# Hashed attention and two feed-forward stages: the second half's AV issued in one block, the next pair's mask moved behind a score

## Chip, core and metric

The program runs on one core of a Trainium2 chip. The metric is the device time of one execution in microseconds: 554.61 us before the change, the median of three runs (554.46 to 555.11). One execution was profiled; its own time is 554.77 us and the span of its trace, from the first to the last instruction, is 553.1 us.

## What is computed

Attention over 16 heads (2 x 8) of 768 tokens with head size 64, in which a query sees only the keys that fall into the same hash bucket, then a feed-forward block, then a mixture of eight experts. The change lies in the attention alone:

```python
q_bits = (einsum('bhsd,dk->bhsk', q, proj) > 0)      # 6 bits, k_bits likewise
mask = q_bucket[:, :, :, None] == k_bucket[:, :, None, :]
scores = where(mask, scale * matmul(q, k.T), -1e9)
attn = exp(scores - scores.max(-1)); attn /= attn.sum(-1) + 1e-9
out = matmul(attn, v)
```

The output of the heads, as a matrix of 1536 x 512, goes through `h = x @ w_in`, a softmax times h, a layer norm and `@ w_out`, and then through the experts; all of that stays as it was.

## The kernel before

The attention takes the first 205 us or so, the two feed-forward stages the rest. Everything is issued in an order written out by hand: each engine works through its own list, and only semaphores tie the lists together.

Heads go in pairs `j` = 0 to 7, one head in each half of the 128 partitions. A pair has two halves `i` of 384 queries (`HW`), and a half has six chunks `c` of 128 keys (`NC`). For every chunk `score(j, i, c)` (L278) puts eight matmuls (L252) into one PSUM tile: query and key in a high part (`Hq`, `Hk`) and a low part (`Lq`, `Lk`), and a fourth product of the hash features `Fq`, `Fk`, which adds a large number where buckets agree. ScalarE (ACT) writes the exponent of it to one of eight buffers `pt` (L288), and GpSimd (POOL) adds the exponents up for the softmax's denominator (L294, L296). For the row maximum `rowmax` (L256) computes the scores a second time, coarsely (four matmuls), and VectorE (DVE) reduces them (L264). Six of these make a half's maxima; `submax` (L266) sends them by DMA into a row of `Fq`, where they are subtracted in the fourth product. Row maxima run ahead: `scans(m)` in `run` issues the next m of them after each score, by a table of six numbers for each half.

`av(j, i, cs)` (L299) multiplies the exponents by the values (L305), two matmuls for each chunk, one for each head. All 12 of a half (24 in the trace) go to one PSUM tile, `self.xs`; `evac` (L310) then moves it out on ACT (L314, L318). Of PSUM there are four tiles of two banks in rotation (`self.order`). While an AV runs, two of them are taken out: `xs`, and `aside`, in which a piece of a feed-forward weight is taken apart (`convert`, `finish`: ACT L553, DVE L554, L557, L560, then ACT L577 or L569 and DVE L578 or L572). `norm` (L366) multiplies finished output by the reciprocal sums on DVE (L369): 768 columns, but only 384 in pair 1.

`first(j)` runs after chunk 1 of a pair's first half. It issues the AV of the second half of pair j-1, `mask(j + 1)` (L228: four matmuls L234 into two PSUM tiles, then `Fk` by ACT, L241, and `Fq` by DVE, L243) and `turn(j + 1)` (L175: `Hk` and `Hq`, L179, on ACT). `second(j)` does the same for the AV of the first half after chunk 1 of the second half, and makes the hash and the bits for pair j+2, which `mask` reads. `low` (L189) makes `Lk` and `Lq` on POOL.

The three row maxima of pair j+1 that follow in the first half of pair j need `Fk`, `Fq`, `Hk` and `Hq` of pair j+1.

Of the kernel before, what the change touches and what calls it, by code (L numbers as in the profile page):

```python
# [119 lines left out]
class Attention:  # L120
# [257 lines left out]
    def run(self, n, extra, fills):  # L378
        self.last = (n - 1, 1)
        scan = [(j, i, c, kh) for j in range(n) for i in range(2) for c in range(3) for kh in range(2)]  # L380

        def scans(m):
            for x in scan[:m]:
                self.rowmax(*x)
            del scan[:m]

        self.hash(0)
        self.turn(0)
        self.load(1, "qk")
        self.warm(8, cols=P)  # L390
        self.mask(0)
        self.warm(2, D)
        self.turn(1)
        for m in range(NC):
            scans(1)
            self.warm(1, D, HW)
        self.hash(1)
        self.submax(0, 0)
        self.threshold(1)
        scans(1)  # L400
        self.mask(1)
        scans(2)
        self.load(0, "v")
        next(extra)
        half = [tuple(range(NC)), (0, 1, 2), (3, 4, 5)]

        rest = []

        def convert():
            rest.extend(next(extra, []))  # L410
            if rest:
                rest.pop(0)()

        def finish():
            while rest:
                rest.pop(0)()

        def first(j):
            self.submax(j, 1)
            if j + 2 < n and j == 0:  # L420
                self.load(j + 2, "qk")
            if j:
                self.xs, self.aside = self.order[:2]
                del self.order[:2]
            if j:
                convert()
                self.av(j - 1, 1, (0, 1))
            if j + 1 < n:
                if j:
                    self.mask(j + 1)  # L430
                    self.turn(j + 1)
            if j:
                self.av(j - 1, 1, (2, 3, 4, 5))
                if j + 1 < n:
                    finish()
                    self.order += [self.xs, self.aside]
                else:
                    self.order.append(self.xs)
                self.norm(j - 1)
                self.evac(j - 1, 1)  # L440
                if j + 2 < n:
                    self.load(j + 2, "qk")
                if j + 1 < n:
                    self.load(j + 1, "v")
            if j == 0:
                self.load(1, "v")

        def second(j):
            if j + 1 < n:
                self.submax(j + 1, 0)  # L450
                self.low(j + 1, "k", self.nc.gpsimd)
                self.low(j + 1, "q", self.nc.gpsimd)
                fills.pop(0)()
            self.xs, self.aside = self.order[:2]
            del self.order[:2]
            convert()
            self.av(j, 0, half[0])
            if j + 1 < n:
                ps = self.wide()
                if j + 2 < n:  # L460
                    self.hash(j + 2, ps[:, 0])
                self.totals(j, ps[:, 1])
                if j + 2 < n:
                    self.threshold(j + 2)
                self.sums(ps[:, 1])
                if j:
                    finish()
                    self.order[1:] = [self.xs, self.order[1], self.aside]
                else:
                    self.order.append(self.xs)  # L470
            self.evac(j, 0)

        for j in range(n):
            for i in range(2):
                for c in range(NC):
                    self.score(j, i, c)
                    scans(((2, 1, 0, 1, 1, 1), (2, 1, 1, 1, 1, 0))[i][c])
                    if c == 1:
                        (second if i else first)(j)
                    if c == 3:  # L480
                        finish()
                        if j in (0, n - 1):
                            self.order.append(self.aside)
                    if (i, c) == (1, 4):
                        self.recip(j)
                    if (j, i) == self.last:
                        if c == 3:
                            ps = self.wide()[:, 0]
                            self.totals(j, ps)
                            self.sums(ps)  # L490
                        if c == 4:
                            self.aside = self.order.pop(0)
                            convert()
                            self.av(j, 1, half[1])
                        if c == 5:
                            finish()
                            self.order.append(self.aside)
        self.av(n - 1, 1, half[2])
        self.evac(n - 1, 1)
        self.order.sort(key=self.pools.index, reverse=True)  # L500
        self.direct(n - 1, 1)
        for ops in extra:
            for f in ops:
                f()
# [999 lines left out]
```

## Time and profile before

| quantity | value |
|---|---|
| median of three runs | 554.61 us |
| profiled execution, its own time | 554.77 us |
| its span | 553.1 us |
| TensorE (PE) busy | 541.9 us, 98% of the span |
| VectorE (DVE) busy | 388.7 us, 70% |
| GpSimd (POOL) busy | 326.5 us, 59% |
| ScalarE (ACT) busy | 268.7 us, 49% |
| granted TensorE clock, mean | 0.998 of full speed |

A share of busy time is an average over the whole program. The change moves instructions in the attention only, so what it is worth has to be read there, from the order of the instructions on each engine and the waits between them. The matmuls' weight loads have a lane of their own in the trace (PEld), and a gap there is the clearest sign that PE stood still, since the ends of matmuls are modelled.

### The profile page before, as it was taken

How to read it: one execution, taken by the hardware profiler on the slowest of the kernel's cores; microseconds unless marked ns; L12 is line 12 of the kernel's file. 1: busy time of each engine (PE TensorE's matmuls, PEld its weight loads, DVE VectorE, ACT ScalarE, POOL GpSimd, SP SyncE). 2: the span in 40 equal slices, each digit the busy share in tenths (PEclk: the TensorE clock that was granted, in tenths of full speed). 3: DMA queues.
4: the chain of work that ended last, by engine and by line, in shares of the span. 5: the costliest groups of instructions: out<-in, count | busy, mean ns of one | idle time of the engine just before them, and what ended most of it. 6: DMA issues, size and time to landing. Idle time of an engine off the chain costs nothing. (4 is left out here: it accounts for less than half of the span.)

```text
span 553.1 us, 9989 instructions
## 1 busy us (share of the span) xinstructions
PE 541.9 (98%) x3863; PEld 435.2 (79%) x3863; DVE 388.7 (70%) x789; ACT 268.7 (49%) x457; POOL 326.5 (59%) x268
## 2 busy tenths in 40 slices
PE   8899999999999999999999999999999999999995
PEld 4766677766677557888888888998989989899894
DVE  8878789798897667777678777766574663655731
ACT  3556758576676542322233324547346454463530
POOL 5498988989889942110001040347695875957741
PEclk9999999999999999999999999999999999999999
DMA  3555474454644338300000030349818458397201
GB/s 114 134 140 192 130 214 157 117 191 110 221 113 116 106 99 318 146 0 1 1 1 1 0 98 1 114 133 378 283 62 324 158 211 296 130 328 256 78 23 37
DMA packets 48550, 76.49 MB, mean 138 GB/s; under 512 B 11885, under 2 KB 20845, under 8 KB 48496
## 3 DMA queue, kind: packets, MB, share of 16 engines
q1 hardware_dynamic: 43360, 59.90, 33.7%
q10 hardware_dynamic: 2896, 9.57, 5.1%
q0 software_dynamic: 2240, 6.31, 3.3%
q8 instruction: 32, 0.52, 0.4%
q14 instruction: 22, 0.18, 0.1%
HBM read 58.79 MB, written 17.94 MB: 139 GB/s over the span
## 5 line engine op out<-in xcount | busy, mean ns | idle before, releaser
L1181 POOL TENSOR_TENSOR wl<-ws,wh 128x512 fp32r<-128x512 f32 x75 | 107.5, 1466 | 41.0 <-ACT wh L1179 41.0
L294 POOL TENSOR_TENSOR acc<-pt,pt 128x768 f32<-128x768 f32 x46 | 85.4, 1857 | 21.1 <-ACT pt L288 21.1
L264 DVE TENSOR_REDUCE m<-ps 128x2 f32<-128x768 f32 x96 | 88.5, 953 | 8.6 <-PE ps L252 6.1
L288 ACT ACTIVATE pt<-ps 128x768 f32<-128x768 f32 x96 | 76.5, 814 | 35.5 <-PE ps L252 35.4
L1291 PE MATMUL o<-wh,wo 128*128 128x512 f32 x256 | 82.6, 394 | 0.0
L1179 ACT CAST wh<-ws 128x512 fp32r<-128x512 f32 x120 | 66.4, 619 | 6.6 <-DMA ws<-in_moe_w_dram 3.5
L654 POOL TENSOR_TENSOR xl<-xT,xh 128x512 fp32r<-128x512 f32 x12 | 15.5, 1293 | 90.8 <-ACT xh L663 50.4
L305 PE MATMUL ps<-pt,v 128*64 128x385 f32 x384 | 67.2, 493 | 0.0
L1181 DVE TENSOR_TENSOR wl<-ws,wh 128x512 fp32r<-128x512 f32 x45 | 52.2, 1186 | 12.5 <-ACT wh L1179 12.4
L1275 DVE SCALAR_TENSOR_TENSOR wo<-g,wo 128x512 fp32r<-128x512 f32 x32 | 22.1, 691 | 52.6 <-ACT wo L1274 52.6
L296 POOL TENSOR_TENSOR acc<-acc 128x768 f32<-128x768 f32 x30 | 55.5, 1850 | 2.4
L1274 ACT ACTIVATE wo<-g 128x512 fp32r<-128x512 f32 x32 | 19.1, 598 | 75.4 <-PE g L1269 75.4
L1291 PEld LDWEIGHTS o<-wh,wo 128*128 128x128 f32 x256 | 48.1, 188 | 9.7
L305 PEld LDWEIGHTS ps<-pt,v 128*64 128x64 f32 x384 | 25.5, 136 | 31.6 <-issue 31.2
L1291 PE MATMUL o<-wl,wo 128*128 128x512 f32 x128 | 50.2, 392 | 0.0
L672 PE MATMUL h<-wi,xh 128*128 128x512 f32 x192 | 49.5, 399 | 0.0
L672 PE MATMUL y<-wo,lh 128*128 128x512 f32 (+1 forms) x176 | 40.8, 384 | 0.0
L672 PEld LDWEIGHTS h<-wi,xh 128*128 128x128 f32 x192 | 34.9, 188 | 7.4 <-ACT xh L663 0.6
L835 POOL DMA_INDIRECT scratch<-row,slot x12 | 12.0, 999 | 47.5 <-DVE slot L862 22.9
L672 PEld LDWEIGHTS y<-wo,lh 128*128 128x128 f32 x176 | 31.5, 188 | 6.6 <-issue 0.2
L252 PE MATMUL ps<-Hk,Hq 64*128 64x384 f32 x192 | 35.9, 357 | 0.9 <-DVE rb L348 0.4
L252 PE MATMUL ps<-Hq,Hk 64*128 64x384 f32 x192 | 36.0, 364 | 0.6 <-DVE wo L572 0.3
(246 smaller groups left out, 1148.0 us busy)
## 6 DMA issues: line engine op xcount, KB each, us to landing
ws<-in_moe_w_dram SPq DMA_DIRECT2D x32, 1024.0 KB, 9.6
scratch<-zero SPq DMA_DIRECT2D x7, 1030.0 KB, 7.3
r<-scratch SPq DMA_DIRECT2D x16, 257.5 KB, 2.9
raw<-in_moe_w_in_dram ACTq DMA_DIRECT2D x8, 512.0 KB, 5.5
raw<-in_moe_w_out_dram ACTq DMA_DIRECT2D x8, 512.0 KB, 5.8
v<-in_v_dram SPq DMA_DIRECT2D x8, 384.0 KB, 5.6
rd<-rd SPq DMA_DIRECT2D x16, 192.0 KB, 3.4
out_dram<-zero SPq DMA_DIRECT2D x3, 1024.0 KB, 6.6
```

The lines of the kernel that those rows point to most:

```text
L252: self.nc.tensor.matmul(ps[:, h], w[r], x[r], start=(n == 0), stop=(n == len(jobs) - 1), tile_position=(D * h, 0))
L264: nc.vector.tensor_reduce(out=st["m", i][:, c, :, kh], in_=ps, axis=AX.X, op=ALU.max, negate=True)
L288: nc.scalar.activation(out=pt[:, :, 0:HW], in_=ps, func=AF.Exp, scale=0.125)
L294: eng.tensor_tensor(out=acc, in0=st["pt", i, c - 1][:, :, 0:HW], in1=pt[:, :, 0:HW], op=ALU.add)
L296: nc.gpsimd.tensor_tensor(out=acc, in0=parts.pop(), in1=acc, op=ALU.add)
L305: nc.tensor.matmul(st["x", i][D * h:D * h + D, 0:HW + 1], st["v"][:, h, c, :], st["pt", i, c][:, h, 0:HW + 1], start=(c == 0), stop=(c == ...
L672: nc.tensor.matmul(ps, a[:, k, :], w[j](k), start=(n == 0), stop=(n == len(jobs) - 1))
L1179: nc.scalar.copy(hi[:, k, :], t[:, k, :])
L1181: eng.tensor_tensor(out=lo[:, k, :], in0=t[:, k, :], in1=hi[:, k, :].bitcast(F32), op=ALU.subtract)
L1274: nc.scalar.activation(out=hi, in_=ps, func=AF.Relu)
L1275: nc.vector.scalar_tensor_tensor(out=hl[:, 2 * g:2 * g + 2, :], in0=ps, scalar=0.0, in1=hi.bitcast(F32), op0=ALU.max, op1=ALU.subtract)
L1291: nc.tensor.matmul(st["o"][t], h[:, f, t * P:(t + 1) * P], w[:, f % 4, :], start=(f == 0 and n == 0), stop=(f == 7 and n == 2),)
```

## The change

In `first(j)` the AV of the second half of pair j-1 is issued as one block of 12 matmuls (24 in the trace, where each counts twice), where two chunks came ahead of the mask and four behind it. `turn(j + 1)` comes ahead of the AV as before. `mask(j + 1)` leaves `first` and is issued behind the score of chunk 2 of the first half. The table of row maxima of the first half, (2, 1, 0, 1, 1, 1), becomes (2, 1, 0, 0, 2, 1) for j over 0: the first one of pair j+1 now follows the score of chunk 4. It was behind chunk 3. Pair 0 is as it was, and pair 7 has no mask to make, so six masks are moved (those of pairs 2 to 7, in pairs 1 to 6).

```diff
             if j:
                 convert()
-                self.av(j - 1, 1, (0, 1))
-            if j + 1 < n:
-                if j:
-                    self.mask(j + 1)
+                if j + 1 < n:
                     self.turn(j + 1)
-            if j:
-                self.av(j - 1, 1, (2, 3, 4, 5))
+                self.av(j - 1, 1, half[0])
                 if j + 1 < n:
                     finish()
                     self.order += [self.xs, self.aside]
...
                 for c in range(NC):
                     self.score(j, i, c)
-                    scans(((2, 1, 0, 1, 1, 1), (2, 1, 1, 1, 1, 0))[i][c])
+                    if (i, c) == (0, 2) and 0 < j < n - 1:
+                        self.mask(j + 1)
+                    scans((((2, 1, 0, 0, 2, 1) if j else (2, 1, 0, 1, 1, 1)), (2, 1, 1, 1, 1, 0))[i][c])
```

`half[0]` is the tuple of all six chunks. The changed file is two lines shorter, so a line of Weights such as L560 is L558 there.

On PE, in the first half of pair 3, from the last row maximum ahead of the AV to the second score behind it (ps_1317 and ps_1318 are the mask's two tiles). Before:

```order
L252 MATMUL ps_1297<-Fk_1008,Fq_1010 128x384 x2
L305 MATMUL ps_1312<-pt6_101,v_723 64x385 x2
L305 MATMUL ps_1312<-pt7_102,v_723 64x385 x2
L234 LDWEIGHTS tab_170
L234 MATMUL ps_1317<-bits_1182,tab_170 128x384
...
L234 MATMUL ps_1318<-bits_1182,tab_170 128x384
L305 MATMUL ps_1312<-pt0_95,v_723 64x385 x2
...
L305 MATMUL ps_1312<-pt3_98,v_723 64x385 x2
L252 MATMUL ps_1354<-Hq_1014,Hk_1012 128x384 x2
...
L252 MATMUL ps_1364<-Hq_1014,Hk_1012 128x384 x2
```

With the change, at the same place (ps_1354 and ps_1355 are the mask's tiles here):

```order
L252 MATMUL ps_1297<-Fk_1045,Fq_1047 128x384 x2
L305 MATMUL ps_1316<-pt6_101,v_713 64x385 x2
...
L305 MATMUL ps_1316<-pt3_98,v_713 64x385 x2
L252 MATMUL ps_1344<-Hq_999,Hk_997 128x384 x2
...
L252 MATMUL ps_1344<-Fq_1047,Fk_1045 128x384 x2
L234 LDWEIGHTS tab_170
L234 MATMUL ps_1354<-bits_1182,tab_170 128x384
...
L234 MATMUL ps_1355<-bits_1182,tab_170 128x384
L252 MATMUL ps_1364<-Hq_999,Hk_997 128x384 x2
```

The mask left the AV, which is whole now, and stands between the scores of chunks 2 and 3.

On DVE, in the first half of pair 2, from the end of the weight piece to the row maxima of pair 3. Before:

```order
L560 SCALAR_TENSOR_TENSOR ps_992<-raw_838,ps_992 128x512
L243 CAST Fq_1010<-ps_1003 128x768
L578 TENSOR_TENSOR wi1_72<-ps_992,wi0_71 128x512
L369 TENSOR_TENSOR xT_67<-xr_717,rd_932 128x768
L264 TENSOR_REDUCE m0_103<-ps_1062 128x2
```

With the change:

```order
L558 SCALAR_TENSOR_TENSOR ps_992<-raw_838,ps_992 128x512
L576 TENSOR_TENSOR wi1_72<-ps_992,wi0_71 128x512
L369 TENSOR_TENSOR xT_67<-xr_707,rd_932 128x768
L243 CAST Fq_1047<-ps_1040 128x768
L264 TENSOR_REDUCE m0_103<-ps_1072 128x2
```

The copy that makes `Fq` moved behind the second half of the weight piece and behind the norm.

On ACT, in the same place, before:

```order
L553 ACTIVATE ps_992<-raw_838 128x512
L241 ACTIVATE Fk_1008<-ps_1002 128x768
L179 CAST Hk_1012<-k_711 128x768
L179 CAST Hq_1014<-q_709 128x768
L577 CAST wi0_71<-ps_992 128x512
```

With the change:

```order
L179 CAST Hq_999<-q_709 128x768
L575 CAST wi0_71<-ps_992 128x512
...
L318 ACTIVATE xr_1021<-ps_1001,vb_1019 128x384
L288 ACTIVATE pt2_97<-ps_1029 128x2x384
L241 ACTIVATE Fk_1045<-ps_1039 128x768
L288 ACTIVATE pt3_98<-ps_1049 128x2x384
```

The activation that makes `Fk` moved from ahead of the two casts to a place between the exponents of chunks 2 and 3. POOL's list and the queues' lists keep their order.

## Rows read from the trace of the kernel before

**Rows 1.** The page: busy time of each engine over the whole span.
```profile
PE 541.9 (98%) x3863; PEld 435.2 (79%) x3863; DVE 388.7 (70%) x789; ACT 268.7 (49%) x457; POOL 326.5 (59%) x268
```

**Rows 2.** Timeline of PEld (start us, us, engine, line): AV starts, pairs 1, 3, 6.
```profile
40.58 0.20 PEld L305 LDWEIGHTS ps<-pt,v 128*64 128x64 f32 x4 [0.19 <-issue]
...
87.34 0.20 PEld L305 LDWEIGHTS ps<-pt,v 128*64 128x64 f32 x4 [0.19 <-issue]
...
157.46 0.20 PEld L305 LDWEIGHTS ps<-pt,v 128*64 128x64 f32 x4 [0.19 <-issue]
```

**Rows 3.** Timeline of PEld, pair 3: mask, AV resumed, score of chunk 2.
```profile
88.78 0.11 PEld L234 LDWEIGHTS <-tab 64*128 64x128 bf16 x4 [0.60 <-issue]
89.21 0.20 PEld L305 LDWEIGHTS ps<-pt,v 128*64 128x64 f32 x4 [0.32 <-issue]
...
91.95 0.19 PEld L252 LDWEIGHTS ps<-Hq,Hk 64*128 64x128 f32 x2 [0.60 <-ACT Hq L179]
```

**Rows 4.** Timeline of PEld, pair 7: a whole AV block and the score behind it.
```profile
180.18 0.20 PEld L305 LDWEIGHTS ps<-pt,v 128*64 128x64 f32 x4 [0.18 <-DVE m L264]
...
184.21 0.19 PEld L252 LDWEIGHTS ps<-Hq,Hk 64*128 64x128 f32 x2 [0.60 <-issue]
```

**Rows 5.** Timeline of PE, pair 3: score 3, row maximum, score 1, second AV.
```profile
92.76 0.33 PE L252 MATMUL ps<-Hq,Hk 64*128 64x384 f32 x2
...
93.63 0.34 PE L252 MATMUL ps<-Fk,Fq 64*128 64x384 f32 x2
...
97.30 0.34 PE L252 MATMUL ps<-Hq,Hk 64*128 64x384 f32 x2
...
98.44 4.10 PE L305 MATMUL ps<-pt,v 128*64 128x385 f32 x24
```

**Rows 6.** Timeline of ACT, pair 3: two exponents; then behind the second AV.
```profile
93.02 1.52 ACT L288 ACTIVATE pt<-ps 128x768 f32<-128x768 f32 x2 [0.18 <-PE ps L252]
...
102.15 0.58 ACT L577 CAST wi<-ps 128x512 fp32r<-128x512 f32 x1 [2.44 <-DVE ps L560]
102.63 0.17 ACT L314 COPY vb<-ps 128x1 f32<-128x1 f32 x1
102.83 0.58 ACT L318 ACTIVATE xr<-ps,vb 128x384 f32<-128x384 f32 x1
```

**Rows 7.** Timeline of DVE, pair 3, from the weight piece to the row maxima.
```profile
90.31 0.72 DVE L560 SCALAR_TENSOR_TENSOR ps<-raw,ps 128x512 int32<-128x512 int32 x1
90.92 0.97 DVE L243 CAST Fq<-ps 128x768 fp32r<-128x768 f32 x1
92.10 0.69 DVE L578 TENSOR_TENSOR wi<-ps,wi 128x512 fp32r<-128x512 f32 x1 [0.22 <-ACT wi L577]
92.71 1.48 DVE L369 TENSOR_TENSOR xT<-xr,rd 128x768 f32<-128x768 f32 x1
94.11 5.74 DVE L264 TENSOR_REDUCE m<-ps 128x2 f32<-128x768 f32 x6
```

**Rows 8.** Timeline of POOL, pairs 3 and 4.
```profile
91.52 1.85 POOL L294 TENSOR_TENSOR acc<-pt,pt 128x768 f32<-128x768 f32 x1
94.68 1.85 POOL L294 TENSOR_TENSOR acc<-pt,pt 128x768 f32<-128x768 f32 x1 [1.31 <-ACT pt L288]
...
114.88 1.84 POOL L294 TENSOR_TENSOR acc<-pt,pt 128x768 f32<-128x768 f32 x1
```

**Rows 9.** Timeline of POOL and DVE, pair 5; then DVE behind the attention.
```profile
138.28 1.85 POOL L294 TENSOR_TENSOR acc<-pt,pt 128x768 f32<-128x768 f32 x1
139.62 1.32 DVE L369 TENSOR_TENSOR xT<-xr,rd 128x768 f32<-128x768 f32 x1
...
207.07 0.89 DVE L369 TENSOR_TENSOR xT<-xr,rd 128x768 f32<-128x768 f32 x1
```

**Rows 10.** Timeline of PE: the matmul behind the mask of pair 1, among row maxima.
```profile
16.38 0.51 PE L252 MATMUL ps<-Hk,Hq 64*128 64x384 f32 x2 [0.36 <-DVE m L264]
```

**Rows 11.** Timeline of PEld, the first score of pair 7.
```profile
177.69 0.19 PEld L252 LDWEIGHTS ps<-Lq,Hk 64*128 64x128 f32 x2 [0.35 <-POOL Lq L193]
```

## The prediction

> **What bounds the kernel now.** I read the page first, then the weight loads of the attention, then DVE, ACT and POOL around one AV block. TensorE is busy for 98% of the span [rows 1], so a change pays if it takes PE time away and costs if it makes PE wait. The attention repeats itself: the AV at the middle of the first half starts at 40.58 in pair 1 and at 157.46 in pair 6 [rows 2], five pairs later, 23.38 us each. One pair therefore stands for six. I take pair 3 and count from the start of its AV, at 87.34 [rows 2]. Three things are to be seen there.
>
> PE does not wait for data in this first half; it only changes over between kinds of matmul. The AV, split by the mask, takes 4.61 us up to the next score (91.95 [rows 3]), with gaps of 0.60, 0.32 and 0.60 in the weight loads. A whole block followed directly by a score takes 4.03 (180.18 to 184.21 [rows 4]).
>
> DVE is nearly full just behind it: weight piece, `Fq`, second part of the piece, norm, then six reductions with no gap from 94.11 on [rows 7]. Their step is 5.74 / 6 = 0.96. The third of them ends at 94.11 + 2.87 = 96.98, and the score that reuses its PSUM tile (chunk 1 of the second half) starts at 97.30 [rows 5]. So the reductions have 0.3 us of slack.
>
> The norm is held by POOL. It ends at 92.71 + 1.48 = 94.19, and POOL's addition, begun at 91.52, ends at 93.37 [rows 7, 8]: 0.82 later. In pair 5 the same difference is 139.62 + 1.32 - 138.28 - 1.85 = 0.81 [rows 9], though the norm started elsewhere. With POOL quiet a norm takes 0.89 [rows 9]. So the norm makes next to no progress while POOL adds, and its end is POOL's end plus 0.82.
>
> **The change, part by part.**
>
> *The AV in one block.* It saves 4.61 - 4.03 = 0.58 for each of six pairs. The mask's own matmuls come back among the scores. PE streams them two by two, as it does the scores, whose steps follow from 92.76 - 91.95 = 0.81 with a slow first one; I take 0.35 for four. Ahead of the AV's second part they took 0.43, with a changeover (88.78 to 89.21 [rows 3]). Net 0.23 saved for each pair, 1.4 in all. Whether the mask needs a changeover among scores is not shown: behind a mask among row maxima PE stood for 0.36, put down to a reduction [rows 10]. Bounds 0 and 0.36; I take 0, because that wait has another cause.
>
> The Trainium skill has a rule on this: in "TensorEngine Tiling (Array Packing)", Key Properties, changing the tiling mode drains TensorE, and changing only the tile within a mode does not. The mask's and the scores' rows both have 64 rows by 128 columns, so by it the price is 0, and with the other bound the sum below would be 1.1 higher.
>
> *Where the mask's result goes.* With six AV chunks done, two PSUM tiles return to the rotation, and the score of chunk 2 takes the first. The mask gets the next one and `xs`, which ACT must have evacuated. Behind the second AV that runs 102.15, 102.63, 102.83, and ends at 103.41 [rows 6], 4.97 after 98.44 [rows 5]. The new block has the same order. The score of chunk 2 starts at 4.03 and lasts 0.81, so the mask could go at 4.84 and its second tile at 4.97 + 0.09 = 5.06 (0.09 is the handover from the AV's end, 102.54, to 102.63 [rows 5, 6]). A stall of 0.2 takes back nearly all of the 0.23. Scores of chunks 3 and 4 then run to 6.8 and the first row maximum's feature part is due at 6.95; before, it ran at 93.63 - 87.34 = 6.29 [rows 5]. The new order and the stall together put it 0.66 later.
>
> *`Fq` on DVE.* It ran in the gap before L578, while ACT was late with its part (0.22 still idle [rows 7]). It now comes behind the norm. The weight piece ends at 90.31 + 0.72 - 87.34 = 3.69; ACT's part takes 0.58 [rows 6] and is no longer queued behind `Fk`, so L578 starts at 4.3 and the norm 0.61 later [rows 7], at 4.9.
>
> If POOL is quiet, the norm ends at 5.8 and `Fq`, 0.97 [rows 7], at 6.7: in time for 6.95. The first reduction starts at most 0.48 behind its matmul (94.11 - 93.63 [rows 5, 7]; the norm had part in that, and I take 0.4), at 7.35. The third ends at 10.2, the score reusing its tile starts 0.1 to 0.2 later, and the second AV 1.14 behind that (98.44 - 97.30 [rows 5]): 11.5. It was 11.10. **The pair grows by 0.4.**
>
> If POOL adds as it does now, to 93.37 - 87.34 = 6.03, the norm ends at 6.85 and `Fq` at 7.74 (a follower starts 0.08 ahead of the norm's end, 94.11 against 94.19 [rows 7]), 0.8 to 0.9 too late. The matmul with `Fq` as its weights runs at 7.9, the first reduction starts at 8.3, the third ends at 11.17, the second AV starts at 12.5. **The pair grows by 1.4.** In general the growth is the norm's end less 5.45.
>
> Which of the two holds depends on the pair before. POOL waits once in a pair, 1.31 for the third exponent [rows 8], and then works without a gap to the end of the addition in question: 114.88 + 1.84 - 94.68 = 22.04 [rows 8]. The third exponent is 0.2 later than before, because `Fk` now comes between two exponents on ACT (its data come 0.58 earlier, but a step of 0.76, 1.52 / 2 [rows 6], is put in). So POOL's addition ends at 6.03 + 0.2 less what the pair before has grown by. With the norm's 0.82 and the 5.45: growth = 1.6 - growth of the pair before, and never under 0.4. Pair 1 has the short norm and grows by 0.4, then 1.2, 0.4, 1.2, 0.4, 1.2 for pairs 2 to 6: 4.8 in all. The split between neighbours may come out evener; two neighbours give 1.6 together in any case.
>
> The Trainium skill's "GPSIMD Engine Reference", Key points, says that GpSimd shares its SBUF interfaces with VectorE and contends with instructions of two SBUF inputs, which the norm is; the rows agree. Were the norm free of it, all six pairs would grow by 0.4, 2.05 in the sum.
>
> *What gets it back.* The first score of pair 7 waits 0.35 for POOL's `Lq` [rows 11]. With pair 6 longer by more than the 0.2 this wait is gone: -0.35. In the second halves nothing changes. The last reduction ends about as far behind the second AV as before (1.4), and DVE idles there for its next input. Behind the attention PE is the bound again, so the delay stays to the end. DMAs, POOL's and SP's lists keep their order; `submax`'s DMA comes later by the growth and is needed only after several scores.
>
> The sum: 4.8 - 0.35 = 4.45. Against the profiled execution's 554.77 that is 559.2; the median of the runs is 0.16 lower, so **559.1**. The handovers are known to a tenth or two, so two neighbours may give 1.2 to 2.0 in place of 1.6: 3.3 to 5.7 in the sum, 557.9 to 560.3.
>
> **The rivals.**
>
> *The norm is not held where it now stands.* Then all pairs grow by 0.3 to 0.5: 1.45 to 2.65 more after the 0.35, about 556.7. For it: the norm starts 0.43 earlier, and POOL may have finished when pairs are longer. Against it: 0.81 and 0.82 in two pairs.
>
> *Not slower: PE's changeovers are all that counts.* If the reductions can start 0.7 later without holding the second AV, the growth is -0.23 for each pair, less up to 0.2 of it for the evacuation of `xs`. This decides at one point: the third reduction must be done 9.6 us after the AV's start, so the first has to begin by 6.8, before its own matmul is due (6.95). It would need more than the two tiles of slack that the rotation gives, or an order of tiles other than I count. The time: -1.4, and +0.4 because pair 7 would wait longer for `Lq`, so 553.6, or up to 554.6 with the `xs` stall.
>
> *The mask drains PE among scores.* 0.36 more in pairs whose `Fq` is in time (three), hidden behind the late `Fq` in the others: +1.1, 560.2; on both sides of the mask, up to 561.
>
> **How the numbers follow.** The forecast gets 64%, the free norm 12%, not slower 18%, the drain 6%. A measurement of this kernel can tell about 0.2% from no change, 1.1 us. Of the 18%, 8 end below 553.5 and 10 within the bound; all others lie above 555.7. So faster 0.08, same 0.10, slower 0.82. The range takes in the forecast, the free norm and the drain: 555.6 to 561.0, and leaves out not slower, 18%, with a little on top.
>
> **What would show it.** In the new trace the AV blocks are 4.03 long. PE waits for ACT L318 at the mask, some 0.2; in every second pair or so PE waits for `Fq` by several tenths ahead of a row maximum, and six times for a DVE reduction ahead of the second half's scores. The norms end 0.82 behind POOL's addition wherever it still runs. The distance from one first-half AV to the next is 23.8 to 24.6, and from pair 1's to pair 7's it is 4.45 more than the 139.60 of before [rows 2, 4]. The forecast is wrong if that distance is 23.4 or less, if PE has no wait for DVE between the mask and the second AV, or if the first reduction starts within 6.8 us of the AV's start.

## The result and the profile after the change

The changed kernel takes 560.00 us (median of four runs, 559.25 to 561.16), the kernel before 554.86 us on the same chip (four runs, 554.46 to 555.80): a ratio of 1.0087 with a 95% interval of 1.0073 to 1.0101. It is slower, by 5.1 us where 4.45 were forecast. The profiled execution took 560.36 us with a span of 558.6; before it was 554.77 and 553.1. The granted clock is 0.997, before 0.998.

The page shows nothing of it: PE is as busy as before, by share [rows 1].

```profile
PE 545.2 (98%) x3863; PEld 437.0 (78%) x3863; DVE 392.5 (70%) x789; ACT 267.3 (48%) x457; POOL 325.3 (58%) x268
```

The weight loads do. The starts of the AV in the first halves of pairs 1, 2, 3, 6 and 7, to be held against [rows 2, 4]:

```profile
40.58 0.20 PEld L305 LDWEIGHTS ps<-pt,v 128*64 128x64 f32 x4 [0.18 <-issue]
...
64.24 0.20 PEld L305 LDWEIGHTS ps<-pt,v 128*64 128x64 f32 x4 [0.19 <-issue]
...
88.64 0.20 PEld L305 LDWEIGHTS ps<-pt,v 128*64 128x64 f32 x4 [0.19 <-issue]
...
161.62 0.20 PEld L305 LDWEIGHTS ps<-pt,v 128*64 128x64 f32 x4 [0.19 <-issue]
...
185.64 0.20 PEld L305 LDWEIGHTS ps<-pt,v 128*64 128x64 f32 x4 [0.85 <-DVE m L264]
```

From pair 1 to pair 7 the distance is 145.06, where it was 139.60: 5.46 more, the whole of the loss (the span grew by 5.5). Pair 1 grew by 0.28, pairs 2 to 6 by 1.02, 0.95, 0.95, 0.96 and 0.95, and the border to pair 7 by 0.35. Inside a pair all of the growth lies between its first AV and its second; the table under the experiments has that distance for every kernel.

The PEld timeline of pair 3, from the score behind the AV to the second AV [rows 3, 5], shows what PE does there:

```profile
92.67 0.19 PEld L252 LDWEIGHTS ps<-Hq,Hk 64*128 64x128 f32 x2 [0.60 <-issue]
...
93.47 0.30 PEld L234 LDWEIGHTS <-tab 64*128 64x128 bf16 x4 [0.16 <-issue]
...
96.14 0.25 PEld L252 LDWEIGHTS ps<-Fk,Fq 64*128 64x128 f32 x2 [0.58 <-DVE Fq L243]
...
100.69 0.20 PEld L305 LDWEIGHTS ps<-pt,v 128*64 128x64 f32 x4 [0.19 <-issue]
```

The AV takes 92.67 - 88.64 = 4.03, the mask fits in among the scores, and then PE waits for `Fq`, here and in each of pairs 2 to 6. Why `Fq` is late stands in the DVE timeline of the same pair [rows 7]:

```profile
92.98 0.69 DVE L576 TENSOR_TENSOR wi<-ps,wi 128x512 fp32r<-128x512 f32 x1 [0.65 <-ACT wi L575]
93.58 1.64 DVE L369 TENSOR_TENSOR xT<-xr,rd 128x768 f32<-128x768 f32 x1
95.14 0.94 DVE L243 CAST Fq<-ps 128x768 fp32r<-128x768 f32 x1
96.70 5.30 DVE L264 TENSOR_REDUCE m<-ps 128x2 f32<-128x768 f32 x6 [0.61 <-PE ps L252]
```

and in that of POOL [rows 8]:

```profile
85.15 1.85 POOL L294 TENSOR_TENSOR acc<-pt,pt 128x768 f32<-128x768 f32 x1 [0.60 <-ACT pt L288]
...
92.56 1.84 POOL L294 TENSOR_TENSOR acc<-pt,pt 128x768 f32<-128x768 f32 x1
96.10 1.84 POOL L294 TENSOR_TENSOR acc<-pt,pt 128x768 f32<-128x768 f32 x1 [1.70 <-ACT pt L288]
```

POOL's addition ends at 92.56 + 1.84 = 94.40, the norm at 93.58 + 1.64 = 95.22, again 0.82 later, and `Fq` stands behind it. The instruction ahead of the norm, L576, also has two inputs, but one of them lies in PSUM; it takes 0.69 here beside POOL's addition, and 0.69 in e10 below (92.22), where POOL ends at 92.32. The first reduction starts 8.06 behind the AV's start, where it was 94.11 - 87.34 = 6.77.

### The profile page after: what moved, and what is told of

Its sections match the earlier page's. It is cut to its first block, busy times and chain, and to the rows that moved or that the text cites. A ratio compares the mean times of both kernels' runs of the same rounds, so it can differ in the third digit from the quotient of the medians.

```text
span 558.6 us, 9983 instructions
## 1 busy us (share of the span) xinstructions
PE 545.2 (98%) x3863; PEld 437.0 (78%) x3863; DVE 392.5 (70%) x789; ACT 267.3 (48%) x457; POOL 325.3 (58%) x268
## 5 line engine op out<-in xcount | busy, mean ns | idle before, releaser
L264 DVE TENSOR_REDUCE m<-ps 128x2 f32<-128x768 f32 x96 | 87.0, 953 | 11.2 <-PE ps L252 10.1
L305 PE MATMUL ps<-pt,v 128*64 128x385 f32 x384 | 65.8, 491 | 0.6 <-DVE m L264 0.6
L1179 DVE TENSOR_TENSOR wl<-ws,wh 128x512 fp32r<-128x512 f32 x45 | 53.5, 1215 | 10.6 <-ACT wh L1177 10.4
L252 PE MATMUL ps<-Hq,Hk 64*128 64x384 f32 x192 | 38.6, 381 | 0.5 <-DVE wo L570 0.3
L252 PE MATMUL ps<-Hk,Hq 64*128 64x384 f32 x192 | 37.3, 371 | 0.9 <-DVE rb L348 0.4
```

The lines of the kernel that those rows point to most:

```text
L252: self.nc.tensor.matmul(ps[:, h], w[r], x[r], start=(n == 0), stop=(n == len(jobs) - 1), tile_position=(D * h, 0))
L264: nc.vector.tensor_reduce(out=st["m", i][:, c, :, kh], in_=ps, axis=AX.X, op=ALU.max, negate=True)
L305: nc.tensor.matmul(st["x", i][D * h:D * h + D, 0:HW + 1], st["v"][:, h, c, :], st["pt", i, c][:, h, 0:HW + 1], start=(c == 0), stop=(c == ...
L1179: eng.tensor_tensor(out=lo[:, k, :], in0=t[:, k, :], in1=hi[:, k, :].bitcast(F32), op=ALU.subtract)
```

## Experiments

The theory, A: DVE is late with `Fq` because the norm now stands ahead of it and is held by POOL's addition. The rivals: the loss comes from PE's own new order (the AV in one block, the mask among scores, the first row maximum a chunk later), or from the norm's place alone, whatever POOL does. The runs came in three series, each on one chip with its own runs of the kernel before (median 555.41, 556.81 and 556.92 us), so ratios are compared across series and microseconds only within one. In the distances, columns 1 to 6 are a pair's first AV to its second, from the timelines of the profiled executions; the border is pair 6's second AV to pair 7's first. The stretches between, from a second AV to the next pair's first, take 12.26 to 12.28 in the kernel before and the changed one; single ones are longer in other profiles (12.93 behind pair 3 of e1) and are not listed.

| kernel | median, us | ratio, 95% interval | pairs 1 to 6 | border |
|---|---|---|---|---|
| before | 554.86 | 1 | 11.10 or 11.11 | 11.61 |
| changed | 560.00 | 1.0087 (1.0073 to 1.0101) | 11.38 12.13 12.05 12.06 12.07 12.06 | 11.96 |
| e1 | 556.67 | 1.0022 (1.0010 to 1.0034) | 11.39 11.39 11.38 11.54 11.40 11.39 | 11.63 |
| e3 | 559.07 | 1.0069 (1.0047 to 1.0091) | 11.65 11.65 11.66 11.73 11.74 11.72 | 11.39 |
| e4 | 575.29 | 1.0355 (1.0335 to 1.0375) | 12.65 15.05 14.84 13.27 14.91 14.86 | 11.91 |
| e6 | 565.38 | 1.0152 (1.0103 to 1.0202) | 12.65 11.51 13.27 14.59 11.57 14.66 | 11.91 |
| e7 | 565.67 | 1.0147 (1.0125 to 1.0169) | 11.92 12.40 14.91 12.14 12.61 12.76 | 13.01 |
| e10 | 562.34 | 1.0121 (1.0088 to 1.0153) | 11.38 11.39 11.39 11.62 11.54 12.39 | 12.00 |
| e13 | 560.94 | 1.0068 (1.0049 to 1.0087) | 11.56 12.05 12.55 12.05 12.04 12.34 | 11.30 |
| e14 | 559.80 | 1.0054 (1.0036 to 1.0073) | 11.37 11.38 11.36 11.53 11.39 11.39 | 12.69 |
| e10b | 560.28 | 1.0071 (1.0051 to 1.0091) | 11.40 11.39 12.11 11.62 11.57 12.28 | 12.55 |
| changed, again | 561.83 | 1.0093 (1.0078 to 1.0109) | 11.38 12.17 12.36 12.06 12.04 12.05 | 12.39 |
| e15 | 555.32 | 0.9982 (0.9969 to 0.9996) | 11.10 or 11.11 | 11.62 |
| e16 | 556.91 | 1.0007 (0.9997 to 1.0018) | 11.38 to 11.40 | 11.50 |

**e1: the norm behind `Fq`.** In the changed kernel the norm alone moves back, behind the mask's copies; AV block, mask and table stay.

```diff
-                self.norm(j - 1)
+                if j + 1 == n:
+                    self.norm(j - 1)
...
                     if (i, c) == (0, 2) and 0 < j < n - 1:
                         self.mask(j + 1)
+                        self.norm(j - 1)
```

> The changed kernel with one thing moved on DVE: the norm (L369) comes behind the copy that makes Fq, no longer ahead of it. Theory A (Fq is late because it queues behind a norm that POOL holds): no wait for Fq is left, the norm falls into POOL's pause and takes about 0.9 us, and pairs 2 to 6 grow by 0.3 to 0.45 us against the kernel before, where they grew by 0.95 to 1.02; in all about 557.3 us (556.6 to 557.8). Rival B (the mask's place on PE and its tiles cost the time, DVE's order nothing): 559.5 to 560.5, as the changed kernel.

Every pair of the profile grows by 0.28 (pair 4's 11.54 apart), a little under the expected 0.3, and most of the loss is gone. DVE and POOL in pair 2:

```profile
70.13 0.69 DVE L578 TENSOR_TENSOR wi<-ps,wi 128x512 fp32r<-128x512 f32 x1 [0.65 <-ACT wi L577]
71.35 0.96 DVE L243 CAST Fq<-ps 128x768 fp32r<-128x768 f32 x1 [0.52 <-PE ps L234]
72.22 0.95 DVE L369 TENSOR_TENSOR xT<-xr,rd 128x768 f32<-128x768 f32 x1
...
69.80 1.85 POOL L294 TENSOR_TENSOR acc<-pt,pt 128x768 f32<-128x768 f32 x1
73.27 1.86 POOL L294 TENSOR_TENSOR acc<-pt,pt 128x768 f32<-128x768 f32 x1 [1.62 <-ACT pt L288]
```

The norm now falls into POOL's wait (71.65 to 73.27) and takes 0.95. The rival of PE's own order is refuted for all but the 0.28, since that order is unchanged here. Whether POOL or the norm's place is the cause, this run can't tell: it moves both.

**e10: POOL's addition kept away from the norm.** DVE's and PE's lists stay as in the changed kernel. In the first halves of pairs 1 to 6 the sum leaves out chunk 1 and takes chunk 2 twice, so this kernel's output is not the program's; the additions are as many and as large as before.

```diff
-        if c % 2:
+        late = i == 0 and 0 < j < self.last[0] and c in (1, 2)
+        if c == 2 if late else c % 2:
...
-            eng.tensor_tensor(out=acc, in0=st["pt", i, c - 1][:, :, 0:HW], in1=pt[:, :, 0:HW], op=ALU.add)
-            if c > 1 and (j, i) != self.last:
+            eng.tensor_tensor(out=acc, in0=st["pt", i, c - 2 if late else c - 1][:, :, 0:HW], in1=pt[:, :, 0:HW], op=ALU.add)
+            if c > 2 and (j, i) != self.last:
```

> The changed kernel, with nothing moved on DVE or PE. POOL's addition of chunks 0 and 1 of the first halves of pairs 1 to 6 adds chunks 0 and 2 instead, so it can't start before the exponent of chunk 2 (5.9 us behind the AV's start) and is not running when the norm starts. Theory A (POOL's addition holds the norm): the norm takes 0.9 to 1.0 us, Fq starts 0.7 to 0.9 earlier, a pair grows by 0.3 to 0.4 in place of 0.95; 556 to 557.5 us. Rival B (the norm's place in DVE's list costs whatever POOL does, or the AV block itself does): 559.5 to 560.5 us.

DVE and POOL in pair 3:

```profile
92.22 0.69 DVE L577 TENSOR_TENSOR wi<-ps,wi 128x512 fp32r<-128x512 f32 x1 [0.65 <-ACT wi L576]
92.83 0.95 DVE L370 TENSOR_TENSOR xT<-xr,rd 128x768 f32<-128x768 f32 x1
93.69 0.95 DVE L243 CAST Fq<-ps 128x768 fp32r<-128x768 f32 x1
95.30 5.30 DVE L264 TENSOR_REDUCE m<-ps 128x2 f32<-128x768 f32 x6 [0.65 <-PE ps L252]
...
90.50 1.82 POOL L297 TENSOR_TENSOR acc<-acc 128x768 f32<-128x768 f32 x1
93.89 3.67 POOL L295 TENSOR_TENSOR acc<-pt,pt 128x768 f32<-128x768 f32 x2 [1.57 <-ACT pt L288]
```

The norm stands where the change put it, and with POOL waiting it takes 0.95 in place of 1.64; pairs 1 to 3 grow by 0.28. So in these pairs it is the hold, and not the norm's place. Pairs 4 to 6 grow by 0.51, 0.43 and 1.28; in pair 6 the norm waits 0.79 for its input `rd`, and what lengthens the other two is not shown. The profiled execution has a span of 556.5, but the median of 562.34 (558.24 to 565.78) misses both expectations.

**e10b and the changed kernel again**, on one chip, to see where the median went.

> The kernel of e10 once more, beside the changed kernel on one chip: in e10 the profiled execution was shorter by what the theory wanted, the median of the timed ones was not. Theory A (the norm held by POOL is most of the loss): at least 2.5 us under the changed kernel's median, and AV to AV 23.65 us for a pair. Rival (the late DMA of the sums takes the gain back in most executions): within 1.5 us of the changed kernel.

> The changed kernel itself, for the comparison on one chip: 1.007 to 1.010 of the kernel before.

e10b is 1.55 us under the changed kernel, just past the rival's bound and short of the theory's. Its profile shows both at work. Pairs 1 and 2 grow by 0.28; in pair 3 the norm waits for another releaser:

```profile
93.62 0.96 DVE L370 TENSOR_TENSOR xT<-xr,rd 128x768 f32<-128x768 f32 x1 [0.65 <-DMA rd<-rd]
```

`rd`, the reciprocal sums by which the norm multiplies, is late. Ahead of `Fq`, the norm passes that wait on to PE as well (12.11 in pair 3). In e1 the norm has no such wait in pairs 2 to 6. In this third series the changed kernel's norm waits 0.89 for `rd` in pair 3 too, and takes 0.96 there, since POOL had finished by then. How much of the missing gain of e10 and e10b is `rd` in the executions that were not profiled is not shown.

**e6: the norm ahead of the second part of the weight piece**, so that it starts earlier.

```diff
                 if j + 1 < n:
+                    self.norm(j - 1)
                     finish()
                     self.order += [self.xs, self.aside]
                 else:
                     self.order.append(self.xs)
-                self.norm(j - 1)
+                if j + 1 == n:
+                    self.norm(j - 1)
```

> The changed kernel with the norm issued earlier on DVE, ahead of the second part of the weight piece (L578), right when the first part ends, while POOL adds for some 2 us more. Theory A (a norm makes no progress while POOL adds): it starts 3.7 us after the AV's start and is 2.8 to 2.9 us long, its end still 0.82 behind POOL's; L578 behind it ends at 7.2, the score of chunk 3, which needs its PSUM tile, waits 2 us, and pairs grow by about 2.2: some 567.7 us (566 to 569). Rival C (the two share, each at a part of its speed): the norm is 1.6 to 1.9 long and ends by 5.6, L578 by 6.2, pairs grow by about 1.0: 559.5 to 561.5.

Two kinds of pair came out, here pair 2 and pair 3, DVE and POOL:

```profile
69.32 1.22 DVE L369 TENSOR_TENSOR xT<-xr,rd 128x768 f32<-128x768 f32 x1
...
93.56 2.52 DVE L369 TENSOR_TENSOR xT<-xr,rd 128x768 f32<-128x768 f32 x1 [0.36 <-DMA rd<-rd]
...
69.67 2.57 POOL L294 TENSOR_TENSOR acc<-pt,pt 128x768 f32<-128x768 f32 x1
...
93.44 1.82 POOL L294 TENSOR_TENSOR acc<-pt,pt 128x768 f32<-128x768 f32 x1
```

In pair 3 POOL is first: two additions (from 91.66 and 93.44) follow each other, and the norm, begun at 93.56, ends at 96.08, 0.82 behind the second. In pair 2 an addition ends at 69.72, and the norm ends 0.82 behind that, at 70.54; now POOL's next addition, which started beside it, takes 2.57 in place of 1.84. Whichever gets in first goes on and the other stands. The length of 2.8 to 2.9 was not reached: in pairs 3, 4 and 6 `rd` came later than I took, and in 2 and 5 POOL's addition ended soon after the norm's start.

The price was larger than the delay of `Fq`: the score of chunk 3 takes the PSUM tile `aside`, and waits there for the weight piece behind the norm. PE stands for 1.6 to 1.7 us in pairs 3, 4 and 6. In 4 and 6 the granted clock then falls to 0.50 (1.2 GHz) for 3.4 us, 0.3 and 0.8 us after the matmuls have resumed, as in e4, next. The median, 565.38, lies between the two expectations, under A's 566 and over C's 561.5. What speaks for A is the norm's end, not the time.

**e4: the kernel before, with only `Fq` behind the norm.**

```diff
-    def mask(self, j):
+    def mask(self, j, late=False):
...
+                elif late:
+                    self.copy = lambda t=t, p=ps[x]: nc.vector.tensor_copy(t, p)
...
-                    self.mask(j + 1)
+                    self.mask(j + 1, True)
...
                 self.norm(j - 1)
+                if j + 1 < n:
+                    self.copy()
```

> The kernel before (AV split, mask in its middle, old table), only with the copy that makes Fq issued behind the norm on DVE, as the change has it. Theory A: the slowdown appears without any move on PE. Fq ends 7.4 to 7.5 us after the AV's start, its matmul runs at 7.5 in place of 6.3, and pairs 2 to 6 grow by 1.1 to 1.2, pair 1 by 0.6: about 561.5 us (560.5 to 562.5). Rival B: 554.4 to 555.4, as the kernel before.

It has the sign of A, and fails on the size: 20 us. PE in pair 3:

```profile
97.61 0.44 PE L254 MATMUL ps<-Hq,Hk 64*128 64x384 f32 x2
...
100.49 0.44 PE L254 MATMUL ps<-Hq,Hk 64*128 64x384 f32 x2 [1.91 <-DVE Fq L243]
...
102.42 0.53 PE L254 MATMUL ps<-Fq,Fk 64*128 64x384 f32 x2
102.74 0.53 PE L254 MATMUL ps<-Hk,Hq 64*128 64x384 f32 x2
...
105.47 0.34 PE L254 MATMUL ps<-Lq,Hk 64*128 64x384 f32 x2
105.64 0.34 PE L254 MATMUL ps<-Hq,Lk 64*128 64x384 f32 x2
```

What waits is not the row maximum but a score, of chunk 3: it takes the PSUM tile that the copy to `Fq` empties. I had counted the data of `Fq` and not its tile. Behind the wait the steps are 0.32 in place of 0.175. The windows of that stretch (wait, then three stretches behind it; the granted clock is the column PEclk):

```profile
core 0: us, PE busy (x) PEld busy (x) DVE busy (x) ACT busy (x) POOL busy (x), PEclk, DMA share, GB/s
98.60:100.40 1.80, 0.00 (x0) 0.00 (x0) 1.80 (x2) 0.81 (x1) 0.15 (x1) 1.00 1.00 374
100.49:101.80 1.31, 1.31 (x14) 1.31 (x16) 0.00 (x0) 0.30 (x1) 0.00 (x0) 1.00 1.00 385
102.10:104.90 2.80, 2.80 (x20) 2.80 (x20) 1.67 (x2) 1.03 (x2) 2.36 (x2) 0.50 0.03 10
105.30:107.80 2.50, 2.50 (x30) 2.35 (x28) 2.20 (x3) 1.43 (x3) 2.50 (x2) 1.00 0.00 0
```

The clock is granted in full (2.4 GHz) while PE stands and for the first 1.3 us after, then at 0.50 (1.2 GHz), then in full again. From 101.82 to 105.29 eleven steps take 3.47, where at 0.175 they would take 1.93: 1.5 us on top of the wait's 1.9. Together they are most of the 3.7 by which this pair grew. Pairs 2, 5 and 6 have such a stretch at 0.50 too and grow by 3.75 to 3.94; pair 4 has the wait without it and grows by 2.16. So the slower clock is some 6 of the 20 us, an estimate of four times 1.5.

**e7: the changed kernel with the old table**, (2, 1, 0, 1, 1, 1) for all pairs.

> The changed kernel with the old table of row maxima, (2, 1, 0, 1, 1, 1): the first row maximum of the next pair stands behind the score of chunk 3 again, and the norm still ahead of Fq. Theory A (DVE is late with Fq because the norm is held by POOL's addition): Fq comes at the same place, 7.5 us behind the AV's start, so PE stops at the feature part with the score of chunk 4 still queued behind it, stands for about 1.2 us there and has 0.7 more to do afterwards. A pair of halves grows by 1.6 to 1.9 in place of 0.95; 563.5 to 566 us. Rival B (the later place of the row maxima on PE is what the change pays for): 556 to 558 us.

1.0147 is 0.6% above the changed kernel's 1.0087, the direction of A; B would have been near 1. Pair 5, PEld and DVE:

```profile
149.66 0.28 PEld L252 LDWEIGHTS ps<-Fk,Fq 64*128 64x128 f32 x2 [1.35 <-ACT pt L288]
...
147.20 1.47 DVE L369 TENSOR_TENSOR xT<-xr,rd 128x768 f32<-128x768 f32 x1
148.60 0.94 DVE L243 CAST Fq<-ps 128x768 fp32r<-128x768 f32 x1
```

PE starts 0.12 behind the end of `Fq` (149.54), so that is what it waited for, 1.35, whatever releaser the row names. Pairs 5 and 6 grow by 1.50 and 1.65, as expected or a little under. The others scatter; in pair 3 the norm waits 1.55 for `rd`, PE stands for 2.1, and the granted clock is 0.50 for 3.4 us from 98.03 on. The table of the change is thus not its cost but saves part of it.

**e3: e1 with the old table.**

> As the run before, and the table of row maxima is that of the kernel before, (2, 1, 0, 1, 1, 1), so that the first row maximum follows the score of chunk 3 again. Theory A: Fq is ready 6.6 us after the AV's start, PE waits 0.3 to 0.4 for it, the reductions start at the norm's end, 7.35, and pairs grow by 0.1 to 0.3: about 556.4 us (555.5 to 557.0). Rival B: no faster than the changed kernel, 560 or more, since the row maximum now waits for a mask that is as late as it was.

A miss: 0.54 to 0.63 for each pair, where less than e1's 0.28 was wanted. In pair 5 the feature part of the first row maximum is now the one ahead of its data, here `Fk`, which ACT makes behind the exponent of chunk 2:

```profile
143.32 0.28 PEld L252 LDWEIGHTS ps<-Fk,Fq 64*128 64x128 f32 x2 [0.49 <-ACT Fk L241]
```

So the new place of the mask needs the new table; with the old one PE waits even when DVE is in time.

**e14: what is left in e1.** On top of e1's edit, from pair 1 on one row maximum moves behind the next half's first score.

```diff
-                    scans((((2, 1, 0, 0, 2, 1) if j else (2, 1, 0, 1, 1, 1)), (2, 1, 1, 1, 1, 0))[i][c])
+                        self.norm(j - 1)
+                    scans((((2, 1, 0, 0, 1, 1) if j else (2, 1, 0, 1, 1, 1)), ((3 if j else 2), 1, 1, 1, 1, 0))[i][c])
```

> The changed kernel with the norm behind Fq, and one row maximum moved from behind the score of chunk 4 to behind the first score of the second half: tables (2, 1, 0, 0, 1, 1) and (3, 1, 1, 1, 1, 0) from pair 1 on. What is left of the slowdown with the norm behind Fq is 0.28 for each pair. Theory A (what is left is the second half's score waiting for the third reduction to give back its PSUM tile): that score now reuses the tile of an exponent instead, and a pair grows by 0.1 at most, 554.7 to 555.6 us. Rival (what is left is the mask among the scores and its wait for the evacuated tile): 556.3 to 557.2 us.

The pairs are as in e1, so A is refuted, but not for the rival's reason. The second half's score and the AV behind it, pair 3:

```profile
98.96 0.25 PEld L252 LDWEIGHTS ps<-Fk,Fq 64*128 64x128 f32 x2
99.40 0.19 PEld L252 LDWEIGHTS ps<-Hq,Hk 64*128 64x128 f32 x2 [0.19 <-ACT pt L288]
...
100.68 0.20 PEld L305 LDWEIGHTS ps<-pt,v 128*64 128x64 f32 x4 [0.22 <-DVE m L264]
```

The score no longer waits for a reduction, but for ACT's exponent: its weights come 0.44 behind the ones before them, where the step is 0.175, and that is nearly all of the 0.28. The AV behind it then waits for a reduction, but by 0.03 only (0.22, where an AV that waits for nothing has 0.19). So the wait that was removed had another beside it, on another engine, with the reductions close behind both. In this profile the border took 12.69, with `recip` waiting 2.37 for its DMA (more on it below), and the stretches behind pairs 2 and 3 took 12.83 and 12.90 in place of 12.27. That the ratio above e1's comes from there is likely, and not shown, since one execution was profiled.

**e13: the last clear moved.** `sums` sends the sums by DMA (`rc`, L350), and `recip` (L354, DVE) waits for it; the second halves issue a 1 MB clear (L1411) before that, in pair 6 2.50 us ahead (176.71). Pair 6's clear moves into pair 7.

```diff
-                fills.pop(0)()
+                if j < n - 2:
+                    fills.pop(0)()
...
+                    if (j, i, c) == (n - 1, 0, 3):
+                        fills.pop(0)()
```

> The changed kernel with one 1 MB zero-clear DMA moved from the second half of pair 6 to the first half of pair 7, so that it doesn't run beside the DMA of the sums (rc). Theory: that DMA is longer because it shares the DMA engines with the zero clear; it lands 4.3 to 4.7 us after its issue in place of 5.33, the AV of pair 7 starts 11.3 to 11.5 us after the one before in place of 11.96, and the time is 559.3 to 559.6 us. Rival: the clear is not what sets it; 5.0 to 5.4 us, 11.6 to 12.0, 560.0 us.

The changed kernel at the border, SP's queue and DVE:

```profile
179.21 0.59 SPq L350 DMA_DIRECT2D rc<-rb  x1
...
184.54 0.23 DVE L354 RECIPROCAL rc<-rc 128x12 f32<-128x12 f32 x1 [1.64 <-DMA rc<-rb]
```

and e13:

```profile
180.39 0.60 SPq L350 DMA_DIRECT2D rc<-rb  x1
...
184.00 0.22 DVE L354 RECIPROCAL rc<-rc 128x12 f32<-128x12 f32 x1
```

5.33 from issue to use with the clear beside it, and without it 3.61 with no wait at all, so that it landed sooner than the expected 4.3. The border is 11.30, as expected; pairs 3 and 6 of this profile were late for `rd` (1.08 and 0.75), and the median can't show 0.5.

**e15 and e16: all seven clears moved** into the first halves, behind the score of chunk 3, in the kernel before (e15) and in e1 (e16).

```diff
-                fills.pop(0)()
...
+                    if j and (i, c) == (0, 3):
+                        fills.pop(0)()
```

> The kernel before with its seven 1 MB zero-clear DMAs issued in the first halves, behind the score of chunk 3, in place of the second halves beside the DMA of the sums (rc). Theory: rc lands 3.6 to 4.0 us behind its issue in every pair, the AV of pair 7 starts 11.2 to 11.4 us after the one before in place of 11.61, and the ratio is 0.998 to 0.9995. Rival: the clears collide with the loads of the first halves (rd is late for the norm): 1.000 to 1.003.

> The changed kernel with the norm behind Fq and the zero clears in the first halves as in e15. Six pairs grow by 0.28 each, the border to pair 7 gives back 0.3: ratio 1.001 to 1.0025. Rival (what remained with the norm behind Fq was late DMA and not the pairs): 0.999 to 1.000.

In both, `recip` never waits for `rc` in pairs 0 to 6; one of e15's:

```profile
128.55 0.60 SPq L350 DMA_DIRECT2D rc<-rb  x1
...
131.95 0.22 DVE L354 RECIPROCAL rc<-rc 128x12 f32<-128x12 f32 x1
```

e15 is the one kernel faster than the kernel before (and so than both), by 0.04 to 0.31%. Its ratio is the expected one, not by the expected way: the border stays at 11.62, because the wait for `Lq` [rows 11] is still there. The profile before, of the first chip, has the same distances; so what e15 gains is what late DMAs cost the kernel before in the third series, and that I infer from the ratio, since no profile of the kernel before was taken there. e16's pairs are e1's, and its ratio, 1.0007, lies between the two expectations. That ratio takes in what the moved clears gain. Against e15, the kernel before with the same clears, e16 is 1.59 us longer (556.91 and 555.32), and from pair 1's AV to pair 7's the profiles have 141.18 and 139.61, 1.57 more: six times 0.28, less 0.12 at the border. That is what is left of the change with the norm behind `Fq`.

## Why the prediction was right, and where its steps failed

**The AV in one block**: 4.03, as counted. **The mask among scores**: the loads flow on behind a gap of 0.16, with no 0.36; the Trainium skill's rule in "TensorEngine Tiling (Array Packing)", Key Properties, that changing only the tile does not drain, agrees with this trace. **The tile `xs`**: ACT emptied it at 93.04 + 0.58 = 93.62, the mask's last matmul starts at 93.83, and in the score behind it one step of the weight loads takes 0.40 (94.20 to 94.60) in place of 0.175, so that the stall of some 0.2 is there.

**The norm held by POOL**: 0.82 behind POOL's end in pairs 2 to 6 of the changed kernel, and 0.95 long in pairs 2 to 6 of e1 and pairs 2 to 5 of e10, where POOL is idle at its start. This, with `Fq` behind it, is the cause of all but 0.28 of a pair's growth: e10 moves nothing but POOL's additions, and in pairs 2 and 3 of its profile 1.02 and 0.95 become 0.28. The Trainium skill's "GPSIMD Engine Reference", Key points, names contention with DVE instructions of two SBUF inputs, and the rows agree. They show how it goes here: one of the two makes next to no progress until the other is done.

**Growth = norm end - 5.45** was too large by 0.2. The norm ends 95.22 - 88.64 = 6.58 behind the AV, which gives 1.13; 0.95 was measured. The reductions' step of 0.96 had been PE's pace. Once they lag behind PE it is 5.30 / 6 = 0.88, and the third ends some 0.2 earlier. The same holds for the quiet case, 0.28 in place of 0.4.

**"Works without a gap to the end of the addition in question"** failed. On it rested growth = 1.6 - growth of the pair before, and the sequence 0.4, 1.2, 0.4. In the changed kernel POOL waits a second time in a pair, 0.60 at 85.15, for an exponent of the second half (0.55 to 0.60 in pairs 2 to 5). That ties POOL to the pair again: its addition ends 5.76 behind the AV in pair 3, and 5.76 or 5.77 in the pairs behind it. So the growth is even, 0.95, and two neighbours give 1.9. Six pairs made 5.11, for 4.8: two errors that nearly cancel, and that the sum of the pairs came so near is luck.

**The 0.35 of pair 7** failed in its sign. The wait for `Lq` did go, but the reductions ahead of the AV stand on DVE behind `recip`, which waited 1.64 for `rc`; the AV, 0.85 behind, came 0.35 later instead of 0.35 earlier. Without the clear, in e13, the border is 11.30, 0.31 under 11.61: the term was right, and a DMA that had been just hidden took its place.

The sum is 5.11 + 0.35 = 5.46 in place of 4.45. Of the rivals, the free norm, priced at 0.3 to 0.5 for a pair and 556.7 in all (a ratio of 1.0038), did not come in this kernel; e1, where the norm is free, has 0.28 for a pair and 1.0022. "Not slower" asked that reductions could start late without holding the second AV; here the first one started at 8.06, and the second AV came 0.95 later. The drain did not show.

## What to carry to other kernels

Before an instruction is moved on one engine, read what the engines beside it do at the place where it lands: the norm, a DVE instruction with both inputs in SBUF, costs 0.95 or 1.64 here, depending on POOL alone, and L576, with one of two inputs in PSUM, takes 0.69 either way. A consumer that PE needs goes ahead of one that nobody waits for. And a tile's release counts as much as its data: in e4 the price was set by the score that needed the PSUM tile.

## What the runs showed of the hardware

- The norm, a DVE instruction with two inputs in SBUF, and POOL's additions exclude each other, in both directions: the norm of 0.95 takes 2.52 where it begins just behind an addition, and POOL's addition of 1.84 takes 2.57 when the norm is first (e6). A norm that POOL holds ends 0.82 behind POOL's end (0.41 for the 384 columns of pair 1).
- In pair 3 of e4, where PE had stood for 1.9 us, the granted clock was 0.50 for 3.4 us, beginning some 1.3 us after the matmuls had resumed: 1.5 us on top of the wait. In its pairs 2, 5 and 6 (stands of 1.9 to 2.1 us) the clock was 0.50 for the same 3.4 us, from 1.2 us after the matmuls had resumed to 0.3 before. In pair 4 a stand of 1.9 us was not followed by it. In e6 such a stretch followed stands of 1.6 and 1.7 us in pairs 4 and 6, and none followed one of 1.7 us in pair 3. What decides between them was not tried.
- In pair 6 a 1 MB clear issued 2.50 us ahead of a small DMA, by the same engine, raised its time from issue to use from at most 3.61 to 5.33 us (e13 and the changed kernel). In pairs 1, 2, 4 and 5 of the changed kernel the clear is issued 3.9 us ahead, and the small DMA is used 3.4 us behind its issue with no wait.
